# A scheduled attention-and-experts kernel with its written order, buffer homes and copy engines replaced

## The chip, the cores and the metric

The kernel runs on one core of one Trainium2 chip. The metric is the time of one execution in microseconds, as the device reports it; lower is better. A core has a matrix engine (PE, with its weight loads shown as PEld), three other compute engines (DVE, ACT, POOL) and a sync engine (SP), which here issues nearly all DMA transfers. PE writes its results into eight PSUM banks, and only DVE and ACT copy them out here.

## The reference

The inputs are q, k and v of shape (8, 8, 576, 64) and the weights of a small mixture of attention experts. The computation, cut to what matters:

```python
# 1. attention inside chunks of 64 rows
scores = (q_c @ k_c.T) / 8; attn = softmax(scores); x = attn @ v_c     # x: (B=8, S=576, 512)
# 2. four experts, each a causal attention of head size 64; the best two of four are mixed
logits = x @ w_gate; w = softmax over the top 2
for e in range(4):
    q, k, v = x @ wq[e], x @ wk[e], x @ wv[e]
    a = softmax(causal(scale * q @ k.T))
    out += w[e] * (a @ v @ wo[e])
```

## The kernel before

Batches are worked through in a software pipeline that is written out by hand, or rather by a planner outside the file. The function builds a list `plan.ops` of 2553 operations, numbered in the order in which `add` was called. An operation names an engine, a closure that issues its instructions, the operations it depends on, the buffers ("slots") it uses, and, for PE, a `form`: how the 128x128 array is split by its matmuls. The forms are `full` (128*128 in the profile), `rows` (64*128), `cols` (128*64) and `quarters` (64*64).

Three strings then decide how that list becomes a program.

- `ORDER` is the sequence of operation numbers in which everything is emitted. Each engine runs its own operations in that order, one queue for each engine. An entry such as `w615` emits 15 matmuls of zeros into PSUM bank 6; they keep PE busy before real work is there.
- `HOMES` gives, slot by slot, which of the physical buffers it lives in (for a PSUM slot: which of the 8 banks).
- `SIDES` has one digit for each of 347 copies that can run on either of two engines: 0 leaves it where it was first named (mostly ACT), 1 takes the other (mostly DVE).

```python
for k in ORDER.split():
    if k[0] == "w":
        for _ in range(int(k[2:])):
            fill(int(k[1]))
        continue
    o = self.ops[int(k)]
    ...
    for u in o.uses:
        key = id(u.pool), u.home
        assert held.get(key, u) is u or held[key].left == 0, "a buffer before it is free"
        held[key] = u
    o.fn()
    retire(o)
```

The PE operations, by the line of the matmul in the profile: L428 scores of the chunks of a group of 128 rows (`quarters`), L331 transposes by the array (`rows`), L503 values of the chunks (`quarters`), L400 `project_v` (`full`, 12 matmuls), L546 `project_qk` (`full`, 12), L647 expert scores (`rows`), L744 expert values (`cols`), L772 `project_out` (`full`, 6). A batch's tall blocks of weights are turned not by PE but by a DMA transpose: POOL copies to `wp` (L338), SP issues the transpose (L342), ACT copies `wpT` to its place (L347). The short blocks are turned by PE (L331, called a turn below) and copied out by ACT (L308) or DVE (L713, L717).

Operations that the later text names: 58, 81 (L503 of groups 0 and 1), 55, 78 (their L331), 56 and 57 (copies of 55's result); 1119 (L744 of batch 1, first pair); 945 and 968 (turns of batch 0, experts 2 and 3), 332 (L503 of group 13), 1253 and 1259 (`project_qk` of batch 2); 2190 and 2213 (turns of batch 6), 2367 and 2376 (scores of batch 7); 2410 and 2433 (turns of batch 7, experts 0 and 1), 2454 (scores of batch 7), 1872 and 2092 (`project_out` of batches 4 and 5); 489 and 634 (L503), 779 (L503 of groups 34 and 35), 1274 (scores of batch 2).

Of the kernel before, what the change touches and what calls it, by code (L numbers as in the profile page):

```python
# [129 lines left out]
63 40 5 109 43 10 25 w48 69 20 70 72 86 w62 46 71 73 8 49 74 47 135 9 50 48 66 75 51 132 76 52 77 13 53 0 28 54 w615  # L130
115 23 116 29 112 55 118 201 78 117 57 119 56 24 79 120 15 58 80 92 164 121 61 59 81 14 62 122 60 82 167 93 796 123 83
170 94 3 84 95 4 85 138 89 797 96 124 207 141 812 97 126 125 139 18 98 784 140 19 99 813 142 30 814 143 100 790 35 785
144 786 145 127 791 146 792 818 128 173 130 129 131 147 819 101 148 176 102 103 149 33 820 104 177 383 34 150 107 179
105 798 210 153 108 151 238 155 106 38 178 157 278 39 180 213 799 181 152 800 154 244 214 182 821 801 281 216 183 156
190 217 815 822 158 184 215 823 218 191 161 816 817 185 192 219 920 163 902 162 186 922 220 923 921 221 907 250 926
908 924 227 927 903 802 275 251 195 222 909 312 252 910 793 228 253 223 803 904 905 805 925 254 911 804 794 189 795
806 229 787 808 918 255 914 912 807 915 916 256 809 196 788 913 789 919 257 160 810 247 197 842 159 204 845 199 264
843 833 226 198 258 200 824 917 838 836 232 265 1032 840 827 839 259 266 841 831 844 837 1000 811 834 848 835 1033 849
829 260 1034 830 846 287 1001 951 825 832 952 1002 233 954 847 352 873 288 962 874 828 290 318 346 877 236 1015 234
263 878 241 237 284 875 235 571 269 879 1038 319 291 876 1017 955 321 1016 320 880 1041 956 906 322 1039 826 953 928  # L140
289 323 884 1035 850 1042 929 324 292 885 851 1043 325 1009 895 854 886 1036 855 293 852 1003 856 883 1037 861 857 294
1040 1012 1004 1010 853 889 872 862 1006 1013 1011 930 863 1005 1014 326 860 295 358 1007 1008 931 890 359 420 296 867
892 891 1021 893 866 360 389 939 870 894 869 361 297 871 327 868 1044 1023 362 1022 932 1018 328 363 1051 933 1049
1045 1052 1047 364 1062 1050 270 1020 1048 1063 1019 365 1065 1064 301 315 271 1024 896 273 392 1046 1053 372 272 897
300 1066 899 1025 1060 1067 898 1068 331 1054 1058 302 274 1056 1069 1253 1026 303 934 973 1055 1057 963 950 935 968
900 945 1028 1254 332 970 947 948 971 946 964 901 1059 1259 969 333 306 337 957 334 338 349 339 938 940 958 949 307
340 1255 1027 1061 366 1260 335 1131 941 310 1261 1093 1029 336 308 1094 1122 311 967 466 309 1143 367 386 1123 961
1262 1129 373 1030 368 1138 1124 1130 1125 1031 1136 1139 1127 1256 1132 1134 944 1097 972 374 1070 1071 1096 1135
1081 1140 1257 1137 395 1142 1073 1128 1258 1072 1263 1146 1126 1075 977 494 398 1147 1074 1264 426 377 399 1104 1171
396 1098 1133 1172 974 1141 371 1095 1228 397 1082 1115 975 400 1105 1083 1234 976 978 1144 1076 1229 401 1106 1145  # L150
# [695 lines left out]
```

## Time and profile before

| what | us |
|---|---|
| median of 3 runs | 374.88 (374.31 to 375.41) |
| the profiled execution's own time | 375.85 |
| its span, first to last instruction | 374.1 |
| PE busy | 365.5 |
| DVE, ACT, POOL busy | 302.7, 284.0, 271.8 |

The sums of the prediction are made against the profiled execution, whose own time is 0.97 above the median. A busy PE is not PE at its peak: matmuls overlap, and a matmul's end is modelled, so the distance from one matmul's start to the next tells more than the busy share.

### The profile page before, as it was taken

Reading aid. Unit: us, or ns where it says so; the run is one execution under the profiler, and the core shown is the slowest. Engines: PE = TensorE matmul, PEld = TensorE weight load, DVE = VectorE, ACT = ScalarE, POOL = GpSimd, SP = SyncE. Lnnn points to the kernel's source line nnn. Section 1 sums busy time; section 2 is a strip of 40 time slices with the busy share of each in tenths; the row PEclk is TensorE's granted clock in tenths of the full one; section 3 lists DMA queues with packets and bytes.
Section 4 is the critical chain, followed back from the end, with each engine's and each line's share of the span. In section 5 each row is a group of like instructions: output and inputs, shape, how many; then the busy total and the mean of one; then the engine's idle time right before and its main releaser. Section 6 shows DMA issues by size and latency. Waiting matters only on the chain.

```text
span 374.1 us, 13090 instructions
## 1 busy us (share of the span) xinstructions
PE 365.5 (98%) x5007; PEld 310.9 (83%) x5007; DVE 302.7 (81%) x1031; ACT 284.0 (76%) x675; POOL 271.8 (73%) x481
## 2 busy tenths in 40 slices
PE   7999999999999999999999999999999999999996
PEld 3699999978888799897998799978798789787675
DVE  2889999899878997979996989389996866976841
ACT  2545799698977995895957979788986759988441
POOL 6754879987998189689777469878598069989600
PEclk9999999999999999999999999999999999999999
DMA  7988779989779996368999698349976404146854
GB/s 259 389 283 282 183 147 263 157 172 170 200 133 191 233 211 144 87 128 221 228 279 167 159 211 154 71 116 176 167 114 93 93 30 89 34 80 135 184 188 168
DMA packets 114222, 63.51 MB, mean 170 GB/s; under 512 B 94576, under 2 KB 94832, under 8 KB 114160
## 3 DMA queue, kind: packets, MB, share of 16 engines
q1 hardware_dynamic: 114016, 62.42, 71.5%
q8 instruction: 39, 0.64, 0.7%
q10 hardware_dynamic: 144, 0.26, 0.2%
q14 instruction: 23, 0.19, 0.2%
HBM read 30.42 MB, written 9.44 MB: 107 GB/s over the span
## 4 chain that ended last, share of the span: by engine, by line
PE 77%; DMA 6%; ACT 5%; POOL 5%; DVE 3%; issue 2%; SPq 0%; DVEq 0%; POOLq 0%
PE bank L546 21%; PE bank L772 14%; PE bank L400 12%; PE bank L744 10%; PE bank L647 9%; DMA wpT<-wp 5%; PE bank L428 5%; PE bank L503 4%; PE bank L331 2%; ACT at L670 2%; POOL wp L338 2%; ACT aT L347 1%; POOL at L692 1%; DMA qs<-in_qt_dram 1%; POOL en L456 1%
## 5 line engine op out<-in xcount | busy, mean ns | idle before, releaser
L692 POOL TENSOR_SCALAR at<-at,st,gate 128x192 f32<-128x192 f32 (+4 forms) x160 | 94.9, 603 | 10.3 <-DVE st L683 9.1
L670 ACT ACTIVATE at<-at,st 128x320 f32<-128x320 f32 (+4 forms) x160 | 88.1, 554 | 8.8 <-DVE st L658 8.0
L347 ACT ACTIVATE aT<-wpT 128x768 uint16<-128x768 uint16 (+1 forms) x64 | 66.8, 1058 | 14.4 <-DMA wpT<-wp 14.0
L546 PE MATMUL bank<-xh,wqk_hi 128*128 128x320 f32 (+1 forms) x256 | 71.9, 303 | 0.8 <-ACT aT L308 0.8
L546 PE MATMUL bank<-xh,wqk_lo 128*128 128x320 f32 (+1 forms) x256 | 70.1, 296 | 0.0
L338 POOL COPY wp<-at 128x768 uint16<-128x768 uint16 (+1 forms) x64 | 58.2, 927 | 12.2 <-DMA wpT<-wp 12.0
L658 DVE CUSTOM_DVE_ANT_0 at<-bank,mask 128x448 f32<-128x448 f32 (+4 forms) x160 | 60.2, 420 | 5.0 <-PE bank L647 4.8
L546 PEld LDWEIGHTS bank<-xh,wqk_hi 128*128 128x128 f32 x256 | 48.4, 189 | 3.3 <-ACT aT L308 0.9
L456 POOL TENSOR_TENSOR en<-e,mx 128x512 f32<-128x512 f32 x36 | 37.1, 1042 | 18.5 <-DVE mx L447 8.5
L546 PEld LDWEIGHTS bank<-xh,wqk_lo 128*128 128x128 f32 x256 | 48.4, 189 | 0.3
L744 PE MATMUL bank<-aT,vv 128*64 128x448 f32 (+4 forms) x384 | 48.3, 393 | 0.1
L744 PEld LDWEIGHTS bank<-aT,vv 128*64 128x64 f32 x384 | 26.1, 137 | 22.3 <-issue 14.4
L546 PE MATMUL bank<-xl,wqk_hi 128*128 128x320 f32 (+1 forms) x256 | 44.5, 296 | 0.0
L347 ACT ACTIVATE et<-wpT 128x1024 uint16<-128x1024 uint16 x31 | 36.2, 1177 | 6.6 <-DMA wpT<-wp 6.6
L727 DVE STREAM_TRANSPOSE aT<-at 32x96 f32<-32x96 f32 x128 | 34.5, 269 | 6.4 <-POOL at L692 2.4
L546 PEld LDWEIGHTS bank<-xl,wqk_hi 128*128 128x128 f32 x256 | 37.7, 190 | 0.0
L400 PE MATMUL bank<-wvg_hi,xh 128*128 128x260 f32 x128 | 33.8, 295 | 0.0
L338 POOL COPY wp<-en 128x1024 uint16<-128x1024 uint16 x31 | 31.6, 1036 | 1.7 <-DMA wpT<-wp 1.3
L438 DVE TENSOR_REDUCE mx<-bank 128x8 f32<-128x512 f32 (+1 forms) x44 | 24.9, 585 | 9.8 <-PE bank L428 9.7
L647 PE MATMUL bank<-kh,qh 64*128 64x288 f32 (+3 forms) x192 | 32.1, 328 | 0.2 <-DVE aT L717 0.2
L400 PE MATMUL bank<-wvg_lo,xh 128*128 128x260 f32 x128 | 32.2, 283 | 0.0
L670 ACT ACTIVATION_READ_ACCUMULATOR at<-at,st 128x1 f32 (+1 forms) x160 | 30.4, 190 | 0.0
(111 smaller groups left out, 851.8 us busy)
## 6 DMA issues: line engine op xcount, KB each, us to landing
ks<-in_kt_dram SPq DMA_DIRECT2D x36, 256.0 KB, 4.3
vs<-in_vt_dram SPq DMA_DIRECT2D x36, 256.0 KB, 4.2
qs<-in_qt_dram SPq DMA_DIRECT2D x35, 256.0 KB, 4.9
out_dram<-y SPq DMA_DIRECT2D x35, 256.0 KB, 2.3
wpT<-wp SPq DMA_TRANSPOSE x95, 3.3
at<-in_wqk_dram SPq DMA_DIRECT2D x4, 256.0 KB, 5.2
at<-in_wvg_dram SPq DMA_DIRECT2D x2, 260.0 KB, 5.5
at<-in_wo_dram SPq DMA_DIRECT2D x2, 256.0 KB, 5.2
```

Source lines behind the costliest of these rows:

```text
L338: pool.tensor_copy(p.t[:, :256 * n].rearrange("p (x n) -> p x n", x=2), src().bitcast(U16).rearrange("p (n x) -> p x n", x=2))
L347: act.activation(put().bitcast(U16).rearrange("p j (q x) -> p j q x", x=2), pt.t[:, :256 * n].rearrange("p (x j q) -> p j q x", x=2, j=n), ...
L400: pe.matmul(bk.t[0:rows, :W_VG], xp[:, k, cols], wp[:, k, :], start=(n == 0), stop=(n == 3 * KT - 1))
L456: pool.tensor_tensor(en.t.rearrange("p (s h k) -> p s h k", s=2, h=HP), ev, rv.to_broadcast([128, 2, HP, 64]), op=OP.mult)
L546: pe.matmul(bk.t[:, :c1 - c0], wp[:, k], xp[:, k, c0:c1], start=(n == 0), stop=(n == 3 * KT - 1))
L647: pe.matmul(bks[s].t[:rows(i), at:at + c1 - c0], q[own, cs], k[own, c0:c1], start=(x == 0), stop=(x == 2), skip_group_check=True)
L658: dve.tensor_tensor_reduce(out=a.t[:r, A_OFF[i] + c0:A_OFF[i] + c1], in0=bk.t[:r, at:at + w], in1=mask[:r, m0:m0 + w], scale=1.0, scalar=f ...
L670: act.activation(af, af, AF.Exp, scale=-1.0, bias=st.t[:r, 0, i, 0:1], accum_out=st.t[:r, 1, i, 0:1])
L692: pool.tensor_scalar(af, af, st.t[:r, 2, i, 0:1], gt.t[:r, i, e:e + 1], op0=OP.mult, op1=OP.mult)
L727: dve.transpose(dst, src)
L744: pe.matmul(bk.t[64 * s:64 * s + 64, c0 - h0:h1 - h0], vs.t[:, j, 64 * (2 * pair + s):64 * (2 * pair + s) + 64], ts[s].t[:, 448 * j + c0:4 ...
L772: pe.matmul(bk.t[:, n0:n1], up[:, k, 128 * t:128 * t + 128], wp[:, k, n0:n1], start=(n == 0), stop=(n == 5), skip_group_check=True)
```

## The change

No operation is added or removed and no closure is altered. The three strings are replaced. In the new ones the fill of the first wait has 9 matmuls and not 8, 155 of the 347 free copies change their engine (163 and not 158 are marked 1), and both the sequence of all operations and the homes of all slots are new. The diff, cut to the lines that the text speaks of (each engine's queue follows from these lines):

```diff
 ORDER = """
-63 40 5 109 43 10 25 w48 69 20 70 72 86 w62 46 71 73 8 49 74 47 135 9 50 48 66 75 51 132 76 52 77 13 53 0 28 54 w615
-115 23 116 29 112 55 118 201 78 117 57 119 56 24 79 120 15 58 80 92 164 121 61 59 81 14 62 122 60 82 167 93 796 123 83
...
-900 945 1028 1254 332 970 947 948 971 946 964 901 1059 1259 969 333 306 337 957 334 338 349 339 938 940 958 949 307
...
-1176 1231 1148 1173 1230 1077 1175 402 1235 1086 979 1099 1243 1236 409 1232 1149 1092 1100 1109 403 1087 1244 1110
-1080 1233 995 410 1114 1111 1090 1113 1091 1088 1112 1089 1103 404 411 1237 996 1150 1153 405 500 1238 1182 1116 503
-1119 1152 501 1117 504 1174 502 534 1118 1159 505 997 414 506 1151 980 1120 1177 408 1170 1160 1178 1225 981 1193 1183
...
-2195 2278 2333 2285 2346 2206 2334 2213 2279 2252 2190 2327 2214 2216 2193 2367 2217 2254 2194 2328 2192 2262 2347
-2189 2191 2376 2215 2368 2372 2256 2374 2385 2369 2377 2253 2375 2379 2219 2277 2222 2387 2373 2276 2386 2378 2348
...
-2413 2428 2406 2433 2461 2434 2436 2435 2437 2421 2455 2462 1872 2459 2457 2429 2398 2460 2438 2458 2422 2092 2456
...
+63 40 20 66 109 43 10 w49 69 25 70 72 135 w62 46 71 73 86 23 47 49 74 24 48 50 132 75 51 76 52 77 0 53 15 13 54 w615
+115 112 28 116 14 5 55 118 78 117 57 119 29 56 120 79 58 80 201 121 81 61 59 62 92 84 60 89 82 122 85 796 123 167 93
...
+900 945 968 963 947 1056 949 969 970 958 898 972 1057 1058
+332 1060 1026 1028 1027 901 1253 306 497 337 964 1054 338 333 1061 973 940 307 335 961 334 934 941 1254 1259 310 336
...
 HOMES = """
-0123110231111673200020100000156332471303465122345021235750011200111246002012203330711021110007411300231021322010007333
...
+2103111231111672300000100000147331561303214122345021227760021300113553003012203332011000012114011000167020322110050333
...
 SIDES = """
-0000000000001101010001001100000010010011110010001010101001000100101001000111001110001000110000110001000110001110100100
...
+0000000010001100100011000000000000000000101110101011011000000010011110011001101000111010010000100000011110010110000011
...
```

The other places that the text names, in the new ORDER (pieces of it, in order):

```
... 1106 1087 1148 1229 1111 409 1113 500 1088 ... 1243 1091 ... 995 403 ... 1239 505 1150 1153 996 506
... 1119 1240 ...
... 2334 2328 2285 2190 2183 2213 2192 2277 2191 2367 2345 2214 2216 2276 2193 2215 2346 2254 2194 2376 ...
... 2466 2428 2454 2469 2467 2470 2405 2429 2459 2433 2461 2460 2434 2468 2092 2398 2436 ...
```

## Rows read from the trace of the kernel before

**Rows 1.** Busy time by engine: us, share of the span, instructions.
```profile
PE 365.5 (98%) x5007; PEld 310.9 (83%) x5007; DVE 302.7 (81%) x1031; ACT 284.0 (76%) x675; POOL 271.8 (73%) x481
```
**Rows 2.** Waits: who waited for whom, us in total, times, longest.
```profile
PEld bank L744 <- ACT aT L347: 1.1, 2, 0.9
PE bank L546 <- ACT aT L308: 0.8, 1, 0.8
```
**Rows 3.** Timeline of PE, 300 to 307: start us, us, engine line op.
```profile
300.15 0.64 PE L400 MATMUL bank<-wvg_hi,xcl 128*128 128x260 f32 x4
...
300.63 0.39 PE L772 MATMUL bank<-wo_hi,uh 128*128 128x512 f32 x1
...
306.01 0.64 PE L400 MATMUL bank<-wvg_hi,xl 128*128 128x260 f32 x4
...
306.57 0.40 PE L647 MATMUL bank<-kh,qh 64*128 64x288 f32 x2
...
306.81 0.29 PE L647 MATMUL bank<-kl,qh 64*128 64x288 f32 x2
...
306.95 0.29 PE L647 MATMUL bank<-kh,ql 64*128 64x288 f32 x2
```
**Rows 4.** Timeline of the start; in brackets the idle time before and its releaser.
```profile
5.67 1.13 PE L428 MATMUL bank<-ks,qs 64*64 64x64 f32 x32 [0.83 <-DMA qs<-in_qt_dram]
...
13.90 0.66 ACT L308 ACTIVATE et<-bank 128x256 f32<-128x256 f32 x2 [1.35 <-PE bank L331]
...
14.60 0.74 DVE L466 COPY et<-bank 128x256 f32<-128x256 f32 x2
...
14.61 0.69 PE L503 MATMUL bank<-et,vs 64*64 64x64 f32 x32 [0.50 <-ACT et L308]
...
16.39 0.39 PE L400 MATMUL bank<-wvg_hi,xh 128*128 128x260 f32 x1
```
**Rows 5.** Window 0 to 28.07: busy us and (instructions) of each engine.
```profile
0.00:28.07 28.07, 25.33 (x473) 18.22 (x474) 18.33 (x52) 11.94 (x24) 18.11 (x50) 1.00 0.89 311
```
**Rows 6.** Timeline of PE at 28 us, after that window.
```profile
28.60 0.58 PE L503 MATMUL bank<-et,vs 64*64 64x64 f32 x25 [0.52 <-issue]
```
**Rows 7.** Chain that ended last, 106 to 115: start us, us, what.
```profile
106.36 4.33 DMA wpT<-wp
...
110.72 0.94 ACT aT L347
...
111.71 2.69 PE bank L744 x15
```
**Rows 8.** Timeline, 84 to 87, PE and ACT.
```profile
84.17 0.72 PE L331 MATMUL bank<-ident,at 64*128 64x64 f32 x16
...
84.82 0.69 PE L503 MATMUL bank<-et,vs 64*64 64x64 f32 x32
85.00 0.37 ACT L552 ACTIVATE qh<-bank 128x256 fp32r<-128x256 f32 x1
85.26 0.97 ACT L308 ACTIVATE aT<-bank 128x128 f32<-128x128 f32 x4
...
86.29 0.39 PE L546 MATMUL bank<-xh,wqk_hi 128*128 128x256 f32 x1 [0.77 <-ACT aT L308]
```
**Rows 9.** Timeline, 338 to 340, PE and ACT.
```profile
338.05 0.30 PE L331 MATMUL bank<-ident,at 64*128 64x64 f32 x2
...
338.51 0.46 PE L331 MATMUL bank<-ident,at 64*128 64x64 f32 x6 [0.16 <-DVE aT L717]
...
338.95 0.71 ACT L308 ACTIVATE aT<-bank 128x128 f32<-128x128 f32 x3 [0.82 <-PE bank L331]
...
339.45 0.49 PE L772 MATMUL bank<-wo_hi,uh 128*128 128x512 f32 x1 [0.48 <-ACT aT L308]
```
**Rows 10.** Timeline of PE, 319 to 320.
```profile
319.63 0.19 PE L647 MATMUL bank<-kh,qh 64*64 64x64 f32 x1
...
320.03 0.24 PE L647 MATMUL bank<-kh,qh 64*64 64x64 f32 x1 [0.21 <-DVE aT L717]
```
**Rows 11.** Groups of DVE by line and form: busy us, mean ns, idle before.
```profile
L658 DVE CUSTOM_DVE_ANT_0 at<-bank,mask 128x448 f32<-128x448 f32 x32 | 19.3, 613 | 0.0
```
**Rows 12.** Timeline of the end.
```profile
370.67 0.76 DVE L777 COPY y<-bank 128x256 f32<-128x256 f32 x2 [4.93 <-PE bank L772]
```

More of the change, by code (lines that the diff above doesn't have):

```diff
@@ L224 @@
-1720034632050110023202210556323112460571010210130221205262610270120043177610710462320034640321021107402102171641231520
-317012102542110562562605122305465720121034300320624506010202032110300463113264250410102132100257135001207241
+2103111231111672300000100000147331561303214122345021227760021300113553003012203332011000012114011000167020322110050333
+1116113001112223100032204100112100000633163110300570010111333271121221030030220333560300001121672223302400010012216100
+0222346120300112157111371110210300601333110250310210212501130014611112103124622233005001212000005033300201030121130057
@@ new lines @@
+1134112012174004013331104611002112101700122204001110032162403620547001012652233371240010012352112067673001145706101120
+0351221212010001150316742204150512253322405670012112200012562051100141602710122145120006057251024042701643134011347542
+3323073121012003221127437251100710364011200401221403011702141307664315101267503322261421100021721200461254001161614510
+1200422100515732125201005173371750206103732230637421002125110213603170011465203011002462102135150113270602512324101770
+2332237416600102105221026753671100430120010210650221373531011200622031640710417224033225712321010026021102160061001474
@@ L226 @@
+115012110350221244230513250503276204111742573223325241102110170202751713001131575710102142100236427061520211
 """
 SIDES = """
-0000000000001101010001001100000010010011110010001010101001000100101001000111001110001000110000110001000110001110100100
-1111010110110001100111001001101100111111000111110000100001101101010010010000111101110000110100010001110100001110000010
-001001110000110111001111111011010101101110011000001011000011101000111100011010110010101110100100010011110001011
+0000000010001100100011000000000000000000101110101011011000000010011110011001101000111010010000100000011110010110000011
@@ L231 @@
+0101101011001111101110110111110111000110100111000001110000111001000001111100101011111000001010111000010101000010000000
+111001001011110011000110011010110010111011000110011101101111101011001101111111000110101101111100111011010000000
 """
```

6 lines of the change are left out of this document (removed), and 158 rows, old and new, of the table ORDER.

## The prediction

> **What bounds the kernel now.** I read the page's busy times first: PE is busy for 365.5 of the span's 374.1 us, the next engine, DVE, for 302.7 [rows 1]. So PE sets the pace nearly everywhere. As a busy PE may still be slow, I then went through the timeline from one matmul's start to the next and compared operations of the same kind. Three kinds of loss come out. (a) Short waits of PE in the middle: few, each about 1 us or less, and of two sorts: for a DMA transpose's last copy, and for a PSUM bank that a copy has not yet left [rows 2]. (b) A toll at each change of the array's split, which nothing lists as a wait. (c) Start and end. The same instructions run after the change, so the time can move only by these three. The largest single waits of (a) add up to some 4 us (worked out below from [rows 7 to 10]), and this caps what a new order can win there.
>
> **The changes of form.** Between two operations of one form, four matmuls of 260 columns take 300.63 - 300.15 = 0.48 us. When a `rows` operation follows, the same four take 306.57 - 306.01 = 0.56, and its first pair then 306.81 - 306.57 = 0.24 where the next takes 306.95 - 306.81 = 0.14 [rows 3]. So this change costs 0.08 + 0.10 = 0.18 us. I walked both ORDER strings, noting the form of each PE operation (fills count as `full`), and counted 138 changes before and 126 after. 12 x 0.18 = **-2.2 us**. Some pairs of forms may pay on one side alone: 12 x 0.10 = -1.2 is the small end, and 12 x 0.20 = -2.4 the large one.
>
> **The start.** The first four loads are issued as before (k and q of group 1, q and k of group 0), so the first matmul, which waits for q, stays at 5.67; the ninth fill lies within the 0.83 us that PE idled there [rows 4] and costs nothing. The weights and v that are reordered behind them have readers that stand after the 15 fills. What does change is the copy 56: it is one of the pair that ACT made from 13.90 to 14.56, and the matmuls of 58 went at 14.61, at its end. Now DVE makes it, behind the four operations on group 3, and DVE came free of these at 14.60, when it began its two copies of 0.37 each [rows 4]. So 58 waits until about 15.0 and 81 until three such copies are done, about 15.75; the L428 operation that filled the gap between 58 and 81 now comes after 81. The first `project_v` (16.39) comes at about 16.95: **+0.55**. Lower bound 0, if PE catches up because a later operation would have waited anyway; upper bound 1.2, if the copies and transposes of group 4, which DVE reaches later too, hold PE once more by the same 0.6.
>
> **The gap at 28 us.** PE stops for 0.52 us in the middle of an L503 operation, with nothing that releases it [rows 6], after 473 + 474 = 947 matmuls and weight loads [rows 5]. I take it for an instruction fetch, which the new order cannot remove: the same count falls into the L428 of groups 5 and 6, also an operation of short matmuls. **0**, or up to -0.5 if PE has to wait there for data anyway. [...]
>
> **The wait for a transpose.** The last one of batch 1's first pair is issued at 106.36, lands after 4.33, ACT copies for 0.94, and PE goes on at 111.71 [rows 7]: 5.35 us. PE's own wait within is up to 1.1 [rows 2]. Between that issue and 1119, PE had two turns, a `project_out`, a `project_v`, a small L503/L428 piece and the short values operation; in the new order it has one turn, the piece, a `project_out` and two `project_v`. One `project_v` is 12 x 0.12 = 1.44 [rows 3]; the turn that falls out is about 0.33 ((84.82 - 84.17) / 2 [rows 8]) and I put the short values operation at the like: +0.8 of cover. **-0.9**, a small rest. Bounds: -1.1, and +1.1 if another transpose becomes as late as this one.
>
> **Bank hand-overs.** A PE operation may start only when the copies of the bank's last owner are done. Three places lose time now.
>
> - 945's bank goes to 1259 with only 332 between: turns end at 84.82, ACT does another copy first, aT copies to 86.23, PE starts at 86.29, 0.77 idle [rows 8]. So 1.45 us were needed. In the new order 332 takes a bank of 945 with one turn between (about 0.4 us of PE work), and 1253 one of 968 with only 332 between (about 0.7).
> - 2433's bank goes straight to 1872: the turn's last matmuls start at 338.51, the copies run from 338.95, PE goes on at 339.45, 0.48 idle, and the turn itself waited 0.16 and its first half 0.46 - 0.10 more for 2410's bank [rows 9]. About 1.0 in all. With ACT free, 0.65 us from the turn's end is what a hand-over takes. The new order puts a whole `project_out` between: gone, -1.0. But 2092 takes a bank of 2454's scores with one turn (0.4 with its change) between, and DVE empties it with a 448-wide copy of 0.61 [rows 11] after a shorter one: about 1.0 needed, +0.6.
> - 2376 stopped for 320.03 - 319.63 = 0.40 [rows 10] with a turn (2190) and 2367 between it and 2213. In the new order only 2367 is left: 0.33 more, +0.3.
>
> The end phase so gives -1.0 + 0.6 + 0.3 = **-0.1** (bounds -1.4, if all three vanish, to +1.0). Batches 0 to 2 (first point): at 0.65 needed, 332 waits 0.25 and 1253 nothing; at 1.45, 1.05 and 0.75. The middle of 0.25 and 1.8 is 1.0 against 0.77 now: **+0.2** (-0.5 to +1.0). Four more hand-overs get about 0.8 to 0.9 us of PE work (489, 634, 779, 1274): nothing at 0.65, about 2.4 together at 1.45; nearer to nothing, as most engines' copies are not late: **+0.4**.
>
> **Copies that change sides.** 80 go from ACT to DVE and 75 back; five more on DVE at 0.3 to 0.7 us are 2 to 3 us of DVE's time, hidden under PE, which works 63 us longer than DVE [rows 1]. They cost only where one stands just ahead of a hand-over, which is counted above. The last two copies go from DVE (0.76 us for both [rows 12]) to ACT: 0.
>
> **Sum.** -2.2 + 0.55 + 0 - 0.9 - 0.1 + 0.2 + 0.4 = -2.05. From the profiled execution's 375.85 that is 373.8; the median of the runs lies 0.97 lower, at 374.88, so the forecast is **372.8 us**.
>
> **The rivals.**
>
> - *The hand-overs become the bound (slower).* I laid PE's operations end to end and read the PE work between the last PE operation on a bank and the next one: below 1.2 us there are 8 such places before and 14 after; below 1.0, 5 and 11. If copies are as late everywhere as at 85 us (1.45 needed), the eleven listed or alike pay 6.9 in all, where the same count gives 4.3 for before and the trace shows 0.77 + 1.0 + 0.4 and some tenths, about 2.6. Then -2.2 + 0.55 - 0.9 + (6.9 - 2.6) = +1.7: 376.6. It decides from about 1.2 us needed per hand-over. For it: the one at 85 us. Against it: the one at 338 us, with ACT free, and that most short distances of before show no wait. [...]
> - *Nothing comes of it.* The changes of form that fall out lie where PE would wait anyway and the small price holds (-1.2), and the start's larger bound is paid (+1.2): 374.9. For it: at the start PE waits for DVE and not for its own work. Against it: from 30 us on PE rarely waits at all.
> - *Nearly all waits go.* -2.2 + 0.55 - 0.5 (gap) - 1.1 - 1.4 - 0.8 = -5.45: 369.4. For it: all of these are single places that an order can move. Against it: an order that is as tight as before's lets new ones in.
>
> **How the numbers follow.** Forecast 0.45 (its own range 371.5 to 373.9), hand-overs 0.20, nothing 0.23, nearly all 0.12. What a measurement of this kernel can tell from no change is about 0.3%, 1.1 us. The forecast's case is nearly all faster by more than that (0.43), with the last rival 0.55; no change takes 0.23 and 0.02 of the forecast's; slower is the hand-overs' 0.20. The range that leaves out no more than 2 in 10 reaches from 369.6 into the slower case at 376.4.
>
> **What would show it.** In the changed kernel's profile: 138 - 12 changes of split, and a `project_v` or `project_qk` of the same length as before where its neighbours have its form; the first `project_v` at about 16.95; a gap of about half a microsecond near the 947th matmul and load; no wait of L744 for ACT's aT near the first pair of batch 1; waits of PE for a bank at 332 and 2092 and none behind 2433. The prediction is wrong if PE's waits for banks add up to much more than 3 us, if a wait for a transpose appears elsewhere, or if the start loses 2 us and not half of one.

## The result, and the profile after

The changed kernel takes **378.12 us** (median of 6 runs, 376.96 to 381.81) where the kernel before takes 374.42 on the same chip: ratio 1.0108, interval 1.0061 to 1.0154. It is 3.7 us slower. The forecast was 372.8, and the range ended at 376.4. The profiled execution took 379.66 with a span of 377.9.

Busy time of the changed kernel by engine, beside [rows 1]:

```profile
PE 364.4 (96%) x5007; PEld 312.7 (83%) x5008; DVE 303.8 (80%) x1036; ACT 284.0 (75%) x670; POOL 272.8 (72%) x481
```

PE works 1.1 us less (365.5 to 364.4), and the span is 3.8 longer, so PE stands still for 13.5 us where it stood for 8.6. The saving is there; the 4.9 us of standing still that came in are more than four times as much. The list of whom PE waited for (us in total, times, longest) names the new ones:

```profile
PE bank L503 <- ACT aT L308: 1.8, 1, 1.8
PE bank L744 <- ACT aT L308: 1.5, 1, 1.5
...
PE bank L428 <- issue: 1.1, 2, 0.6
PE bank L546 <- ACT vv L308: 1.1, 1, 1.1
```

The largest in [rows 2] were 1.1 and 0.8. To count the shorter ones too I took, for each of the 2553 operations that is PE's, the distance from its first matmul to the next operation's first, and compared it with the usual distance for the same kind and the same form before and behind it. The two traces then account for all of the 3.8 us of span:

| us | before | after | difference |
|---|---|---|---|
| PE's operations at their usual distances | 350.39 | 348.03 | -2.4 |
| the fills of the start | 9.16 | 7.92 | -1.2 |
| at 332's banks (84.8 before, 81.4 after) | 0.84 | 2.20 | +1.4 |
| at 1119 | 1.08 | 0.17 | -0.9 |
| end phase: 2376, and the turn 2433 | 1.47 | 0.84 | -0.6 |
| around 634 (244 to 246) | 0 | 0.85 | +0.85 |
| operations in which PE stands with nothing releasing it (28 before; 15 and 194 after) | 0.75 | 1.72 | +1.0 |
| seven places that the prediction did not name (69.7, 93, 166, 215, 249, 282, 296) | 0 | 5.5 | +5.5 |
| smaller ones | | | +0.3 |

The fills' -1.2 belongs to the execution and not to the order. In the profiled execution of before the fills followed one another at 0.43 us up to 9.6 us and at 0.21 only then; in the changed kernel's they come at 0.21 from about 4 us on. So the L428 of group 3, which comes right behind the fills, goes at 12.54 before and at 10.63 after; but it goes at 10.52 in a later kernel that has the old start and a quick execution (before, queues moved, of experiment 4):

```profile
12.54 0.69 PE L428 MATMUL bank<-ks,qs 64*64 64x64 f32 x32
```

```profile
10.52 0.69 PE L428 MATMUL bank<-ks,qs 64*64 64x64 f32 x32
```

The places themselves, in the timeline of the changed kernel (start us, us, engine, line; in brackets the idle time before and its releaser):

```profile
10.63 0.69 PE L428 MATMUL bank<-ks,qs 64*64 64x64 f32 x32
...
12.70 1.08 DVE L466 COPY et<-bank 128x256 f32<-128x256 f32 x3
...
13.17 1.24 PE L503 MATMUL bank<-et,vs 64*64 64x64 f32 x64 [0.40 <-DVE et L466]
...
15.33 0.46 PE L428 MATMUL bank<-ks,qs 64*64 64x64 f32 x14 [0.59 <-issue]
...
15.72 0.39 PE L400 MATMUL bank<-wvg_hi,xh 128*128 128x260 f32 x1
...
69.39 0.76 PE L331 MATMUL bank<-ident,at 64*128 64x64 f32 x16
...
69.82 0.93 ACT L347 ACTIVATE aT<-wpT 128x768 uint16<-128x768 uint16 x1 [0.85 <-DMA wpT<-wp]
...
70.78 0.38 ACT L308 ACTIVATE vv<-bank 64x260 f32<-64x260 f32 x1
...
71.21 0.39 PE L546 MATMUL bank<-xh,wqk_hi 128*128 128x256 f32 x1 [1.06 <-ACT vv L308]
...
81.15 0.98 PE L331 MATMUL bank<-ident,at 64*128 64x64 f32 x16
...
81.64 1.11 DVE L727 STREAM_TRANSPOSE aT<-at 32x96 f32<-32x96 f32 x4
...
83.34 0.28 DVE L757 TENSOR_TENSOR ul<-bank,uh 128x128 fp32r<-128x128 f32 x1
83.44 0.94 ACT L308 ACTIVATE aT<-bank 128x128 f32<-128x128 f32 x5
...
83.94 0.69 PE L503 MATMUL bank<-et,vs 64*64 64x64 f32 x32 [1.81 <-ACT aT L308]
...
111.53 2.40 PE L744 MATMUL bank<-aT,vv 128*64 128x448 f32 x20
...
194.32 0.33 PE L428 MATMUL bank<-ks,qs 64*64 64x64 f32 x3 [0.49 <-issue]
...
293.71 0.71 PE L331 MATMUL bank<-ident,at 64*128 64x64 f32 x16
...
295.99 1.99 ACT L347 ACTIVATE aT<-wpT 128x1024 uint16<-128x1024 uint16 x2 [2.52 <-DMA wpT<-wp]
297.89 0.76 ACT L308 ACTIVATE aT<-bank 128x128 f32<-128x128 f32 x4
298.20 0.44 PE L744 MATMUL bank<-aT,vv 128*64 128x128 f32 x4 [1.46 <-ACT aT L308]
```

How to read it:

- *Start.* The first `project_v` goes at 15.72, not at 16.39 [rows 4], although DVE now makes the copy 56. DVE is not late for it: its copies begin at 12.70, on the heels of PE's turn.
- *69.7.* PE needs a bank whose last owner was a `project_v`. The value copy (vv, 0.38) could have run since 60 us, when its `project_v` was done, but it stands in ACT's queue behind the copy of a DMA transpose, and ACT itself waits 0.85 for that transpose to land.
- *81.4.* The turns end at 82.1. Their copies (aT L308) begin at 83.44, behind ACT's exponentials; DVE's copy out of another of 332's banks (ul L757, 83.34) stands behind four 32x96 transposes of 1.11 us. PE waits 1.81 at once.
- *295.6.* Four copies of a turn that was done at 294.4 wait until 297.89, because ACT is standing for a transpose (2.52).
- *1119* no longer waits.

ACT's waits for transposes, from the list of waits, before and then after:

```profile
ACT aT L347 <- DMA wpT<-wp: 14.0, 14, 3.6
...
ACT et L347 <- DMA wpT<-wp: 6.6, 6, 2.0
```

```profile
ACT aT L347 <- DMA wpT<-wp: 16.7, 18, 2.5
ACT et L347 <- DMA wpT<-wp: 15.8, 11, 4.0
```

ACT stands 32.5 us for them instead of 20.6, and all that is queued behind on ACT stands too.

One more view matters: two stretches with equal PE work, before and then after (window, us, busy of PE, PEld, DVE, ACT, POOL with instructions, granted clock, DMA share, GB/s):

```profile
0.00:67.15 67.15, 63.89 (x1127) 54.76 (x1128) 55.89 (x167) 41.67 (x97) 47.78 (x99) 1.00 0.87 253
67.15:101.80 34.65, 33.88 (x552) 28.35 (x551) 31.94 (x115) 31.95 (x79) 30.32 (x51) 1.00 0.87 183
```

```profile
0.00:65.12 65.12, 61.10 (x1124) 53.95 (x1126) 52.45 (x153) 43.41 (x99) 46.72 (x96) 1.00 0.89 252
65.12:102.42 37.30, 34.27 (x558) 28.72 (x557) 33.77 (x124) 34.02 (x86) 32.33 (x55) 1.00 0.86 190
```

At 65 us the changed kernel leads by 2.0 us; at 102 it lags by 0.6. In the first stretch DVE has done 3.4 us less than before while PE did the same. In the second, ACT, DVE and POOL are each busy for 87 to 92% of the time in both kernels; so the busy share alone does not make the difference. But each of the three has 1.8 to 2.1 us more to do there than before, and PE only 0.4. From there on the changed kernel wins and loses in steps, compared at equal PE work: about half a microsecond ahead at 120 us, 1.2 behind at 200, 2.0 at 295, 3.7 right after the wait at 296, 3.8 at the end.

### The profile page after: what moved, and what is told of

It is laid out like the page before. It is cut to its first block, busy times and chain, and to the rows that moved or that the text cites. A ratio compares the mean times of both kernels' runs of the same rounds, so it can differ in the third digit from the quotient of the medians.

```text
span 377.9 us, 13077 instructions
## 1 busy us (share of the span) xinstructions
PE 364.4 (96%) x5007; PEld 312.7 (83%) x5008; DVE 303.8 (80%) x1036; ACT 284.0 (75%) x670; POOL 272.8 (72%) x481
## 4 chain that ended last, share of the span: by engine, by line
PE 54%; DMA 13%; ACT 11%; DVE 8%; POOL 8%; issue 5%; ACTq 0%; SPq 0%; POOLq 0%; DVEq 0%
PE bank L546 14%; PE bank L772 11%; DMA wpT<-wp 10%; PE bank L744 9%; PE bank L400 8%; PE bank L647 6%; ACT at L670 5%; POOL wp L338 3%; PE bank L503 3%; DVE at L658 3%; PE bank L428 2%; POOL en L456 2%; ACT aT L347 2%; PE bank L331 2%; ACT et L347 1%
## 5 line engine op out<-in xcount | busy, mean ns | idle before, releaser
L692 POOL TENSOR_SCALAR at<-at,st,gate 128x576 f32<-128x576 f32 (+4 forms) x160 | 95.3, 608 | 5.5 <-DVE st L683 3.8
L670 ACT ACTIVATE at<-at,st 64x64 f32<-64x64 f32 (+4 forms) x160 | 88.1, 553 | 11.8 <-DVE st L658 11.6
L347 ACT ACTIVATE aT<-wpT 128x1024 uint16<-128x1024 uint16 (+1 forms) x64 | 66.7, 1057 | 17.3 <-DMA wpT<-wp 16.7
L546 PE MATMUL bank<-xh,wqk_hi 128*128 128x256 f32 (+1 forms) x256 | 72.0, 303 | 1.2 <-ACT vv L308 1.1
L546 PE MATMUL bank<-xh,wqk_lo 128*128 128x256 f32 (+1 forms) x256 | 70.0, 296 | 0.0
L338 POOL COPY wp<-at 128x1024 uint16<-128x1024 uint16 (+1 forms) x64 | 58.3, 930 | 10.5 <-DMA wpT<-wp 10.4
L658 DVE CUSTOM_DVE_ANT_0 at<-bank,mask 128x288 f32<-128x288 f32 (+4 forms) x160 | 60.3, 421 | 1.3 <-PE bank L647 1.2
L546 PE MATMUL bank<-xl,wqk_hi 128*128 128x256 f32 (+1 forms) x256 | 44.5, 296 | 0.0
L647 PE MATMUL bank<-kh,qh 64*128 64x288 f32 (+4 forms) x192 | 32.5, 329 | 0.2
L772 PE MATMUL bank<-wo_hi,uh 128*128 128x512 f32 (+1 forms) x74 | 29.9, 405 | 0.2 <-DVE st L658 0.2
```

Source lines behind the costliest of these rows:

```text
L338: pool.tensor_copy(p.t[:, :256 * n].rearrange("p (x n) -> p x n", x=2), src().bitcast(U16).rearrange("p (n x) -> p x n", x=2))
L347: act.activation(put().bitcast(U16).rearrange("p j (q x) -> p j q x", x=2), pt.t[:, :256 * n].rearrange("p (x j q) -> p j q x", x=2, j=n), ...
L546: pe.matmul(bk.t[:, :c1 - c0], wp[:, k], xp[:, k, c0:c1], start=(n == 0), stop=(n == 3 * KT - 1))
L647: pe.matmul(bks[s].t[:rows(i), at:at + c1 - c0], q[own, cs], k[own, c0:c1], start=(x == 0), stop=(x == 2), skip_group_check=True)
L658: dve.tensor_tensor_reduce(out=a.t[:r, A_OFF[i] + c0:A_OFF[i] + c1], in0=bk.t[:r, at:at + w], in1=mask[:r, m0:m0 + w], scale=1.0, scalar=f ...
L670: act.activation(af, af, AF.Exp, scale=-1.0, bias=st.t[:r, 0, i, 0:1], accum_out=st.t[:r, 1, i, 0:1])
```

## The experiments

All ratios are against the kernel before on the same chip, with 95% intervals. "Changed" is the changed kernel.

**1. Single late copies.** The copies behind eight of the changed kernel's waits are put ahead of what holds them (15 entries of ORDER, one of the lines shown).

```diff
-1005 328 872 1009 885 1001 1036 1002 883 1037 296 886 952 928 1013 358 929 1010 953 1011 331 954 297 890 359 932 867
+1005 328 872 1009 885 1001 1036 1002 1013 883 1037 296 886 952 928 358 929 1010 953 1011 331 954 297 890 359 932 867
```

> The changed kernel with ACT's (and once DVE's) order altered at eight places and nothing else: a copy that empties a PSUM bank goes ahead of an instruction that waits for a DMA transpose or of a row of exponentials. Engines, banks and PE's order stay. Theory (queue): PE's new waits come from copies that stand in line behind something late on their own engine; the waits at 69.7, 81.4, 92 to 93, 165.9, 215, 244, 282 and 295.6 us, 7.8 us together in the profiled run, fall to about 2 to 3, and the time from 378.1 to about 373.5 (372 to 375). Rival (distance): the order leaves too little PE work between two owners of a bank, so PE waits whoever copies first: the same places keep over 5.5 us and the time stays at 377 or more.

Measured: 378.41, 1.0089 (1.0065 to 1.0112). The waits at 69.7, 92, 215, 244 and 282 are gone from the trace, and the time is not: 332 still waits, now for DVE's copy alone, and then something new comes. The timeline, and the windows of that run:

```profile
84.05 1.12 PE L503 MATMUL bank<-et,vs 64*64 64x64 f32 x28 [1.23 <-DVE ul L757]
...
85.48 0.41 PE L546 MATMUL bank<-xh,wqk_lo 128*128 128x256 f32 x1
```

```profile
82.00:84.00 2.00, 0.82 (x12) 0.52 (x10) 1.91 (x8) 1.95 (x10) 2.00 (x4) 0.98 0.70 131
84.00:86.00 2.00, 1.95 (x32) 1.83 (x33) 2.00 (x9) 2.00 (x9) 1.68 (x7) 0.50 0.51 98
86.00:88.00 2.00, 2.00 (x30) 1.87 (x32) 1.58 (x7) 2.00 (x6) 1.92 (x4) 0.67 0.86 216
```

PE was busy for 0.82 of the 2 us from 82 to 84; then the granted clock is at 0.50 from 84 to 86 and at 0.67 from 86 to 88, and a `project_qk` matmul that lasts 0.28 in the changed kernel's own profile lasts 0.41. It does not always come so: in the changed kernel's own profile PE was busy for only 0.19 us from 82 to 84, and the clock stayed at 1.00. That those waits are the loss falls: with five of them gone the kernel is no faster, as others come in.

**2. The sides.** The SIDES string of before in the changed kernel; and, as a smaller dose, five copies given back to their other engine.

```diff
-0000000010001100100011000000000000000000101110101011011000000010011110011001101000111010010000100000011110010110000011
...
+0000000000001101010001001100000010010011110010001010101001000100101001000111001110001000110000110001000110001110100100
...
```

> The changed kernel with the string of sides of the kernel before: all 155 copies that went to the other engine go back, the order and the banks stay. Rival (sides): copies given to ACT made it late; with them back on DVE the waits at 81.4 and 295.6 us, where two of the four or five copies in line were DVE's, fall by half or more and the time to 375.5 or less. Theory (queue): the order was written for its own sides and the copies still stand behind the same transposes and exponentials, now with some on DVE behind DVE's own work: no gain in sum, 377 to 380.

> The changed kernel with five copies at the three worst places (two aT copies at 81 us, one project_qk copy at 244, two aT copies at 296) put on DVE as in the kernel before, order and banks the same. Rival (sides): these five explain the waits at 81.4, 244 and 295.6, 4.4 us together: they fall by 2 or more, 376 or less. Theory (queue): the other copies of the same banks still stand in ACT's line, so 2.2, 0.7 and 1.5 fall by less than 1 in all: 377 to 378.

Measured: 390.9, 1.0433 (1.0405 to 1.0461), and 379.67, 1.0128 (1.0108 to 1.0148). Giving the old sides back wins nothing: the new sides fit the new order. Whether other sides would fit it better was not tried. With the old ones, the two engines wait for each other at the halves of one operation's copies:

```profile
ACT at L670 <- DVE st L658: 17.0, 18, 2.7
...
DVE aT L717 <- ACT aT L308: 8.1, 6, 3.2
...
ACT aT L308 <- DVE aT L717: 3.0, 5, 1.2
```

**3. The start alone.** The first entries of the changed ORDER, with their homes and sides, on the kernel before.

```diff
-63 40 5 109 43 10 25 w48 69 20 70 72 86 w62 46 71 73 8 49 74 47 135 9 50 48 66 75 51 132 76 52 77 13 53 0 28 54 w615
-115 23 116 29 112 55 118 201 78 117 57 119 56 24 79 120 15 58 80 92 164 121 61 59 81 14 62 122 60 82 167 93 796 123 83
...
+63 40 20 66 109 43 10 w49 69 25 70 72 135 w62 46 71 73 86 23 47 49 74 24 48 50 132 75 51 76 52 77 0 53 15 13 54 w615
+115 112 28 116 14 5 55 118 78 117 57 119 29 56 120 79 58 80 201 121 81 61 59 62 92 84 60 89 82 122 85 796 123 167 93
...
```

> The kernel before with only the first 26 us of the changed order (with its banks, sides and 49 fills up to there); all that follows is in the order of the kernel before. The start of the changed kernel led by 0.8 us there and by 2.0 at 33 to 67 us, before its waits began. If the lead comes from the start alone and is kept: 374.4 - 0.8 = 373.6, and 372.9 if the gap of 0.7 us near the 947th matmul and load, which the changed kernel doesn't show, goes as well. Rival (lead is given back at the next landing): 374.4.

Measured: 376.74, 1.0064 (1.0038 to 1.0090). The first `project_v` comes at 15.97, 0.4 earlier than before, and at 23 us the lead is 0.5; then PE waits in an L428 operation, because the order behind is the old one and DVE's copy out of its bank has not been made:

```profile
30.59 0.62 PE L428 MATMUL bank<-ks,qs 64*64 64x64 f32 x26 [0.67 <-DVE xl L518]
```

So a start that is better by itself does not make the kernel faster: PE comes to that bank earlier, DVE does not. This wait explains 0.7 us; what makes up the rest of the 0.64% (2.4 us) was not followed up.

**4. The queues as a whole.** Here the entries of ACT, DVE and POOL are moved among PE's operations, whose own sequence stays: in the changed kernel (61 entries moved; ACT's alone, 33; DVE's alone, 37), and by the same procedure in the kernel before (27); then a second time, chosen anew (62 and 43).

```diff
...
-1050 1045 366 1024 896 303 274 1052 1053 897 950 1046 957 900 945 968 963 947 1056 949 969 970 958 898 972 1057 1058
-332 1060 1026 1028 1027 901 1253 306 497 337 964 1054 338 333 1061 973 940 307 335 961 334 934 941 1254 1259 310 336
+1050 1045 366 1024 896 303 274 1052 1053 897 957 945 968 963 947 1056 949 969 970 958 898 900 972 1057 1058
+332 1060 950 1026 1028 901 1253 306 1046 497 337 964 1054 338 335 961 333 1061 973 940 307 334 934 941 1254 1259 1027 310 336
```

(The place at 81 us alone: 9 entries, of which these lines show six.)

> The changed kernel with 57 instructions put forward or back by some places in the queues of ACT (29), DVE (23), GpSimd (3) and SyncE (2), where the rows of the runs so far show an instruction ready behind one that waits, the eleven moves of ACT in the first experiment among them. PE's order, banks and sides are those of the changed kernel. The first experiment mended seven places and left the largest, at 81 us: there the copy on ACT came early enough, but its bank then waited for a subtraction that stood on DVE behind 1.1 us of transposes. Theory (queues of the copying engines): with both queues mended PE keeps the 2.4 us of fewer changes of form: 378.1 falls to 373 (371.5 to 374.5), below the kernel before, and PE's waits beyond the start from about 14 us to 6 or less. Rival (PE's own order leaves too little between two owners of a bank): the waits stay above 10 us and the time at 377 or more.

> The kernel before with 26 instructions moved in the queues of ACT (8), DVE (10), GpSimd (7) and SyncE (1) in the same way; PE's order, banks and sides as in the kernel before. Its waits beyond the start are about 5 us. Theory: it gains less than the changed kernel does, 374.9 to 373.5 (372.5 to 374.5), since its queues were in better order to begin with; so the mended changed kernel stands at or below it. Rival (PE's order): no gain in either, 374.9.

> The changed kernel with 31 instructions moved in ACT's queue alone. Theory (ACT's queue is the larger part of the loss): 378.1 to 374.7 (373.5 to 376). If the two queues matter only together (a bank is free when the later of its two readers is done): 376.5 or more.

> The changed kernel with 35 instructions moved in DVE's queue alone. Theory (ACT's queue is the larger part): 377 (376 to 378.5), a gain of 1 or 2 us at most. If DVE's queue is the larger part instead: 375.5 or less.

> The changed kernel with 61 instructions moved in the queues of ACT (29), DVE (26), GpSimd (5) and SyncE (1), chosen anew with two things that the earlier runs showed: copies of one bank by ACT and DVE go one after the other in the written order, even where they read different columns, and waits of PE of more than about 1.5 us near 85 and 247 us were followed by some us at the lower clock (0.5 granted). PE's order, banks and sides are those of the changed kernel. Theory (the loss is the order of the copying engines' queues): no wait of PE above 0.8 us after the start, the granted clock stays at 1.0, 378.1 falls to 372.5 (371 to 374.5). Rival (an order can't be mended ahead of the transposes' landings, which differ from run to run): new waits come at other places and the time stays at 377 to 379.5 as in the last four.

> The kernel before with 41 instructions moved in the queues of ACT (10), DVE (24), GpSimd (5) and SyncE (2), chosen in the same manner. Theory: 374.9 to 373.5 (372.5 to 375), above the mended changed kernel by about 1 us, what is left of the 2.4 us of fewer changes of form. Rival (landings): 374.5 to 376.

> The changed kernel with nine instructions moved on ACT and DVE, all of them between 74 and 92 us, so that both banks of the operation at 82 us are emptied early. Theory: PE's waits from 81 to 88 us fall from 2.2 us (over 3 in the first experiment, with the lower clock behind it) to about 1.2, the rest of the profile stays, and the time falls by 1 to 1.5: 376.7 (376 to 378). Rival (landings): another wait between 84 and 110 us takes the place of it, 378 or more.

| kernel | us | ratio | interval |
|---|---|---|---|
| changed, queues moved | 379.48 | 1.0106 | 1.0078 to 1.0134 |
| changed, ACT's alone | 379.50 | 1.0127 | 1.0092 to 1.0162 |
| changed, DVE's alone | 379.26 | 1.0116 | 1.0088 to 1.0144 |
| changed, queues moved again | 377.63 | 1.0080 | 1.0065 to 1.0096 |
| changed, the place at 81 us alone | 377.53 | 1.0079 | 1.0061 to 1.0096 |
| before, queues moved | 375.87 | 1.0025 | 1.0004 to 1.0046 |
| before, queues moved again | 374.34 | 0.9992 | 0.9982 to 1.0002 |

The first set had put copies of one bank by two engines into an order in which they wait for one another, at 245 us:

```profile
245.49 0.29 DVE L517 CAST xh<-bank 128x128 fp32r<-128x128 f32 x1 [1.06 <-ACT xch L308]
...
246.21 0.77 ACT L308 ACTIVATE xh<-bank 128x128 fp32r<-128x128 f32 x2 [0.58 <-DVE xch L517]
...
247.53 0.24 PE L647 MATMUL bank<-kh,qh 64*64 64x64 f32 x1 [0.81 <-DVE xcl L518]
```

These waits are for semaphores of the program. In the second set this is mended. With it the places of 69.7, 81.4 and 244 cost 0.8, 0.7 and nothing, where they cost 1.2, 2.2 and 0.85. The total falls by no more than its interval, since others open: 92 us, 0.98; 111 us (1119 again), 0.97; 122 us, 0.59; 173 us, 0.83. PE is ahead after a repair, and another hand-over is late instead. That a better order of the copies alone gives the gain back is not borne out by any of the five runs of the changed kernel. All five lie above 377, the mark that was set for the rival that PE's own order leaves too little work between two owners of a bank; so they do not rule it out.

**5. The gaps with no releaser.** PE's gaps "issue" stand, in either kernel, behind fixed counts of its matmuls and weight loads. The windows that end at the gaps of the changed kernel count them:

```profile
0.00:15.33 15.33, 11.42 (x219) 6.35 (x221) 8.61 (x25) 6.59 (x12) 10.74 (x43) 1.00 0.88 320
0.00:194.30 194.30, 186.51 (x3008) 161.05 (x3009) 166.22 (x552) 148.38 (x347) 153.73 (x273) 1.00 0.82 200
```

219 + 221 = 440 and 3008 + 3009 = 6017; before it was 947 [rows 5, 6], and other runs have one at 1200. All of these are 440 and a whole number of times 253.5 (2, 3 and 22). Of the many such counts only those show that fall in a long row of 64x64 matmuls or up to 5 us after it.

The traces also show what the gaps go with. Every page lists a queue of instruction packets:

```profile
q8 instruction: 39, 0.64, 0.7%
```

That is 39 packets of 16 KB, and PE has some 10110 instructions in the traces, 39.5 times 256. Counted with the semaphore and drain instructions of PE's queue, the gaps lie at 448, 960, 1216 and 6080 (or one more), which are whole numbers of times 256 apart. In all 20 traces PE never passes one of the counts 448 + n x 256 sooner than 1.2 us after the packet of the same number has ended, and in the gaps it goes on 1.2 to 1.6 us after it: in the changed kernel the packets end at 13.97 and 192.88 us and PE goes on at 15.33 and 194.32; in the kernel before it is 27.10 and 28.60. I read this as PE standing there because its next instructions come late; what the traces hold is the counts and the order of the times. As 64 short matmuls take 1.09 us, a row of 128 with their loads, 256 instructions, is through in 2.2 us by estimate, no longer than a packet (0.88 to 2.35 us in the profiles of the two kernels, most about 1) and the 1.2 us behind it together.

To move the counts, the 26 short fills of the start are replaced by seven long ones that take about the same time. A long fill stands in the trace as two matmuls and two loads, so the count moves by 24, and not by the 38 that the expectations name:

```diff
-63 40 20 66 109 43 10 w49 69 25 70 72 135 w62 46 71 73 86 23 47 49 74 24 48 50 132 75 51 76 52 77 0 53 15 13 54 w615
+63 40 20 66 109 43 10 w42 69 25 70 72 135 w71 46 71 73 86 23 47 49 74 24 48 50 132 75 51 76 52 77 0 53 15 13 54 w64
...
-    warm = sb.tile([128, 512], BF16, name="warm")
+    warm = sb.tile([128, 480], F32, name="warm")
```

> The changed kernel with the 26 fills ahead of the first real work replaced by seven of four times the length each (fp32 in place of bf16), for about the same time: 38 fewer matmuls and weight loads stand ahead of all that follows, order, banks and sides the same. In the runs so far PE stood for 0.5 to 1.3 us, with nothing that releases it, at the same counts of matmuls and weight loads (440, 946, 1200, 6018, that is 440 + n x 253.5) whatever the time of day, where several operations of short matmuls follow one another; in the changed kernel at 14.5 and 193.6 us. Theory (these are fetches of instructions, and bunching the short operations lets PE outrun them): with the count shifted by 38, count 440 falls into a project_v and 6018 into a project_qk, so both gaps go; one may come at count 946, now behind 285 short instructions. 378.1 to 376.9 (376.2 to 377.8). Rival (the gaps belong to the operations or to DMA traffic at that time): they stay in the L428 operations at 14.5 and 193.6 us, 378 or more.

> The last mending of the changed kernel's queues (377.6) with the same seven long fills. Its gaps at counts 440, 946, 1200 and 6018 cost up to 2.9 us in the profiled run. Theory (fetches): 377.6 to 376 (375 to 377), still not below the kernel before unless all four go. Rival: 377.4 or more.

> The kernel before with the same seven long fills: a control for what the fills do by themselves. The gap of 0.7 us at count 947 moves on to an operation behind 221 short instructions, so it may stay. Theory (fetches): 374.5 (373.8 to 375.2). If the long fills hurt the start or the clock, 375.5 or more, and the two runs above are to be read with that.

Measured: changed with long fills 377.64, 1.0075 (1.0046 to 1.0103); with the second set of queue moves as well 377.31, 1.0063 (1.0041 to 1.0086); the kernel before with long fills 374.33, 0.9976 (0.9960 to 0.9993). In the changed kernel the gaps at 15 and 194 are gone, but one has come into the L503 of group 4:

```profile
26.57 0.29 PE L503 MATMUL bank<-et,vs 64*64 64x64 f32 x7
27.72 0.58 PE L503 MATMUL bank<-et,vs 64*64 64x64 f32 x25 [0.86 <-issue]
```

This gap lies again behind 947 matmuls and loads, where other operations stood without the long fills. So these gaps follow the count and can be moved; where one shows, PE is idle for 0.2 to 1.2 us. In the kernel before no gap shows at 28 us with the long fills; but none shows there either in three traces of that order with the short fills (queues moved, queues moved again, and the lighter copies of experiment 6), so that is not the fills' doing, and its 0.24% is not explained by the gap. That trace lacks the wait at 1119 as well (1.08 before).

**6. Lighter copies.** Both kernels with half of the columns in the exponentials (L668), the weights' scaling (L691), the maximum (L439) and the sum (L445). PE's work and the order stay, and the output is no longer the attention of the reference. By busy time this takes 16 to 17 us off ACT, 17 off DVE and 20 to 21 off POOL, less than the 32, 24 and 30 that were expected.

```diff
-                        r, n = rows(i), 128 * i + 64
+                        r, n = rows(i), 64 * i + 32
...
-                af = a.t[:r, o_:o_ + n]
+                af = a.t[:r, o_:o_ + n // 2]
```

> The kernel before with less work on the three engines beside PE and none less on PE: the exponentials of line 668 run over half of their columns, the weights' scaling of line 691 over half, the maximum of line 439 and the sum of line 445 over half of the keys (so the output is not the attention of the reference). This takes about 32 us off ACT, 30 off POOL and 24 off DVE of some 375. It is the measure for the next kernel. Copies theory (PE's waits in both kernels are copies and loads that come late because ACT, DVE and POOL are full): well below before, 369 to 371. Theory of PE's side (what remains is the time PE needs for its matmuls, changes of form and instruction fetch): 373 to 374, since only the 3 us of waits listed for banks and values can go.

> The changed kernel with the same four pieces of work halved. Copies theory: the 12 changes of form that it saves (2.4 us of PE's own work) show once the copying engines have room, so it is 1.5 to 3 us faster than the lighter kernel before, and its excess of waits over that kernel's falls from 7 us to 1 or 2. Theory of PE's side (the regrouping itself costs PE the time, by fetch or by bursts of bank claims that no lighter copy cures): it stays 2 to 3.5 us slower than the lighter kernel before. If only the transposes by DMA matter, whose length this does not change, it is about equal to it (within 1 us).

Measured: before 372.99, 0.9945 (0.9927 to 0.9963); changed 374.17, 0.9983 (0.9965 to 1.0001). Neither theory has it whole. The distance between the two orders falls from 1.08% (4.0 us) to 0.38% (1.4 us): relief of ACT, DVE and POOL is worth 2.1 us to the old order and 4.7 to the new one. The difference, 2.6 us, is known to about 2 us by the intervals. And the new one stays behind. Its lighter trace still holds 1.3 us at 332, and has three gaps with no releaser, where the lighter old order has none:

```profile
33.33 0.41 PE L546 MATMUL bank<-xh,wqk_hi 128*128 128x320 f32 x1 [1.06 <-issue]
...
194.27 0.33 PE L428 MATMUL bank<-ks,qs 64*64 64x64 f32 x3 [0.77 <-issue]
```

So the last run puts the long fills into the lighter changed kernel.

> The changed kernel with the lighter copies of after_lighter (half of the columns of the exponentials, of the weights' scaling, of the maximum and of the sum, so that the output is not the attention of the reference) and the seven long fills of seven_long_fills, which shift the count of PE's instructions. The lighter changed kernel stands at 374.2, 1.2 above the lighter kernel before (373.0), and its trace holds gaps in which nothing releases PE at counts 438, 1198 and 6016 (0.61, 1.37 and 0.98 us, some 2.5 in all above a usual distance of matmuls) where the other's holds none. Theory that the rest of the loss is these gaps: they go or move to where they show less, and the time is 371.8 to 373.0, at or below the lighter kernel before. If one gap stays, as it did in seven_long_fills (1.08 at 26.6 us): about 373.3. Theory that the rest is waits for banks and values: unchanged, 374 to 374.4.

Measured: 373.48, 0.9962 (0.9940 to 0.9984). The gap to the lighter old order shrinks from 0.38% to 0.17%, about 0.6 us, which the intervals don't tell from nothing, nor surely from 0.38%. The gaps at 33 and 194 us are gone, the one at 15 is there still (0.86, at the same count but 12 matmuls further on in its operation), and, as in experiment 5, one has come at 28 (0.86). The trace also holds the wait at the turn of 82.7 (1.3). Some of the rest is the gaps, then; that all of it is, was not shown.

**7. A better kernel.** The kernel before with the second set of its queue moves and the long fills.

> The kernel before with the moves of queues_of_before_again (two places of copies put earlier; 374.34, 0.9992) and the seven long fills of before_long_fills (374.33, 0.9976) together. If the two are independent: 373.8 (373 to 374.6), ratio 0.996 to 0.997. If both only take the same slack: 374.3, 0.998.

Measured: 374.24, 0.9984 (0.9971 to 0.9998). The two don't add up. The best is the kernel before with long fills alone (0.9976), which is hardly more than a measurement can tell.

## Why the prediction was wrong

Point by point, by its own steps.

- **Changes of form, -2.2: right.** At usual distances PE's operations take 2.37 less. The term was sized well, and it is the only one that the order could bank for certain.
- **Start, +0.55: wrong sign.** The first `project_v` comes at 15.96 in the middle of the 14 profiles with the new start, and at 16.2 in the 6 with the old one: some 0.2 earlier. The step that failed is "DVE makes it, behind the four operations on group 3": I took DVE's free time, 14.60, from the profiled execution of before, where the L428 of group 3 ran at 12.54 behind slow fills. With quick fills it ran at 10.52 with the old start and at 10.63 with the new one; after, DVE was through with it at 12.70, and the copies were not late.
- **Gap at 28 us, 0: half right.** It is a matter of the count, as I took it for. But I fixed one count where there is one every 253.5. At 947 no gap shows in the changed kernel's own profile (up to 0.44 us in other runs of its order), and the new order puts rows of short matmuls at two others: +1.0 in all. Nor is the gap at 28 us a steady part of the kernel before: it shows in one of four traces of the old order with the short fills. That PE stands there for its instructions is what the packets of experiment 5 speak for: PE goes on 1.2 to 1.6 us after one has ended. At most of the counts no gap shows; those that show lie in or soon after rows of short matmuls, 0.2 to 1.2 us of idle time each.
- **1119, -0.9: right,** and so was the bound I did not take, "if another transpose becomes as late as this one": PE's values wait 0.55 at 282 and 1.7 at 296.
- **End phase, -0.1:** -0.6; the hand-over to 2092 costs 0.69 as foretold (0.6), 2376 loses less than before (0.15 after 0.41). The first is a plain case of too little PE work between two owners: from the turn to 2092 PE takes 1.02 to 1.03 us in all 13 traces of the new order, whatever was done to the copies.
- **332, +0.2: mis-sized.** It measured +1.4. Even the upper bound (1.05 at a hand-over that needs 1.45 us) was too low: ACT's copies of 945 and DVE's copy out of its other bank, a hand-over that I had not listed, both came late, and PE stood 1.81 at once.
- **Four more hand-overs, +0.4:** one of them, 634, pays 0.85. The sum of 0.4 was low by half a microsecond.
- **What was left out, +5.5.** This is the step that failed: "nearer to nothing, as most engines' copies are not late". I priced only hand-overs that are short in PE's own sequence and put all others at nothing. The waits at 69.7, 93, 166, 215, 249 and 296 are not among the hand-overs I listed. At 69.7 the copy had ten microseconds; it was late because of what stands ahead of it in its engine's queue, above all ACT's copies of DMA transposes, for which ACT stands 12 us longer than before. I had counted copies' durations and PE's distances and never walked ACT's and DVE's queues.

The rival that came nearest is the hand-overs' one (376.6, with 0.20), though for its direction and not for its places. Its condition, copies as late everywhere as at 85 us, is not shown: the changed kernel meets it in some ten places. In its favour, 2.0 us of lead were given back within 37 us, in a stretch where the two engines that empty PSUM are both at 91%. That emptying PSUM was the limit there is not shown by this, as these engines are as busy there in the kernel before (92%).

What is shown: the old sides do not give the loss back (experiment 2), nor do any few copies (1, 4), and it is not in the start, behind which the changed kernel leads by 2.0 us at 65 us. Relieving ACT, DVE and POOL together takes away about 2.6 us, give or take 2, of the 4.0 us between the orders (6). Moving the instruction counts takes away about 0.8 more, by medians whose intervals overlap (5, 6). The sizes are rough, as the changed kernel's own ratio is known to half a per cent only. What stays open: which of the three engines counts most, since they were relieved together; and how much of the 2.6 is DMA transposes that land late because POOL prepares them later, and how much is the copies' own time. A kernel that takes the transposes off ACT's queue would tell, and was not tried. Nor does experiment 6 tell full queues from a PE order that leaves too little between two owners of a bank, as lighter copies also shorten what a hand-over needs; at 2092 it is the latter. The new homes were never tried by themselves.

## What to carry to other kernels

Here 2.0 us of PE's lead were gone after a stretch in which ACT, DVE and POOL were each busy for 87 to 91% of the time: read the stretch, not the whole span, and what each engine has to do in it, before a gain is put into the sum. Price a hand-over by walking the queue of the engine that copies, up to the last thing it waits for; at 69.7 us a copy that could have run ten microseconds before was late behind a DMA's landing. And before single waits are repaired, relieve the suspected engines crudely in both versions: that run told more than seven repairs.

## What the runs showed of the hardware

- PE's gaps with no releaser in or soon after long rows of short matmuls lay at counts of 440 and multiples of 253.5 more of its matmuls and weight loads, or 448 and multiples of 256 with its semaphore instructions, in most profiles; 0.2 to 1.2 us idle. In them PE went on 1.2 to 1.6 us after a 16 KB packet of the instruction queue had ended (15.33 after 13.97 in the changed kernel, 28.60 after 27.10 in the kernel before).
- In the profile of experiment 1 PE was busy for 0.82 us from 82 to 84; the granted clock was then 0.50 from 84 to 86 and 0.67 from 86 to 88, and the 12 matmuls of 1253 took 2.6 us (85.10 to 87.70) where they take 1.6 in the changed kernel's own profile. So this wait cost more than itself. With five sides given back (experiment 2) PE was busy for 0.46 us from 82 to 84, and the clock was 0.50 from 84 to 88 and 0.55 from 88 to 90; with the queues moved (experiment 4) for 0.95 us from 246 to 248, and the clock was 0.56 and 0.58 up to 252. It stayed at 1.00 after the 1.81 us at 81.4 in the changed kernel's own profile. So the "more than about 1.5 us" of an expectation is not a limit that these runs show.
- In these programs DVE's and ACT's copies out of one bank waited for one another by semaphores, 1.06 and 0.58 us at 245 us, and DVE's for ACT's 8.1 us in all with the old sides. Whether the chip would hold them without a semaphore no run shows.
- In the changed kernel ACT's wait of 2.52 us for a DMA transpose to land, up to 295.99, held back four copies of a turn that was done at 294.4; they began at 297.89.
